# Wider vector instructions and more Strassen tiles in a fused attention and ELU feed-forward kernel

## The chip, the cores and the metric

One core of a Trainium2 chip runs the whole program. The metric is the device time of one execution in microseconds (us); the kernel before takes 332.08 us (median of 3 runs, 331.69 to 332.18).

The engines have short names in the profile: PE is TensorE's matmuls, PEld its weight loads, DVE VectorE, ACT ScalarE, POOL GpSimd, SP SyncE. PSUM is the memory that matmuls write to, SBUF the on-chip memory that all engines read.

## What is computed

Attention over 8 batches with 8 heads of 576 tokens, 64 wide. 16 beacon keys and values per head stand ahead of the 576 keys; every query sees the beacons, and the rest causally. The heads' outputs are then 4608 rows of 512, which go through a feed-forward block with an ELU between two matrix products.

```python
k_all = np.concatenate([beacon_k, k], axis=2)      # 16 + 576 keys
scores = scale * np.matmul(q, k_all.transpose(0, 1, 3, 2))
scores = np.where(causal, -1000000000.0, scores)
a = np.exp(scores - scores.max(-1, keepdims=True))
a /= a.sum(-1, keepdims=True) + 1e-09
x = np.matmul(a, v_all)                            # -> (4608, 512)
h = x @ w_in                                       # 512 x 2048, "FFN1"
g = np.where(h > 0.0, h, np.exp(np.minimum(h, 0.0)) - 1.0)
out = g @ w_out                                    # 2048 x 512, "FFN2"
```

## The kernel before, in words

**Steps and their order.** The kernel is a set of small functions ("steps") and one long list of words written out by hand at the end: `F.4.10` calls step F with the arguments 4 and 10. Each step issues a few instructions, and every engine executes its own in the order of the list. Nothing reorders them. A wait on another engine stops what stands behind it on the same engine.

**Attention.** Batch b's keys are cut in 5 chunks of 128 (the last has 80 rows). Step S (L317) computes transposed scores for a piece of columns of one batch, x (L332) takes their exp on ScalarE into the fp16 tile `et`, m (L337) multiplies the diagonal blocks by a triangle on VectorE. `et` holds two heads of one pair p, and two pairs share one buffer. For most groups D (L390) adds the chunks of `et` into one sum per head, so that L (L374, L416) needs one matmul with a vector of ones per head for the softmax denominators. n takes 1/sum on ScalarE by Ln and Exp, W (L374) multiplies with the values, M (L468) scales and writes the transposed activations `xT`. Scores of batches 0 to 2 come by transposes on TensorE (T, L263, copied out by cq and ck, L276), those of later batches by DMA transposes (lt) of a copy in DRAM (lk). Copies and loads that convert (q, k, v, w_in, w_out) are issued on POOL, where step lp also writes a memset (L773) and a copy. The four loads of w_out are the steps wo.0 to wo.3 (L163).

**Feed-forward tiles.** Tokens go in tiles: tile 0 is tokens 0 to 255, tile 1 is 256 to 511, tiles 2 to 9 have 512 tokens each. FFN1 for a block of 128 hidden features (two blocks in tiles 0 and 1) is step F (L508): four matmuls of 512 columns, or eight of 256. ELU is three steps: e (exp, ScalarE, L518), u (relu, on ScalarE at L524, or with `.v` on VectorE at L526), k (VectorE, L536), which writes `min(exp - 1, relu)` into `gt`. r and g are another form of it on VectorE (L543, L548).

**FFN2.** For tiles 2 to 9 it is a Strassen product: 7 products in place of 8 block products, at the cost of block sums. wt forms differences of w_out once, Z (line 578 through the helper `sub`) forms four block sums of `gt` per tile, Q (L624) issues some of the tile's 112 matmuls of 256 columns, J (L633, L638, L640) adds partial results and starts the output's DMA on SP. For tiles 0 and 1, FFN2 is direct: G (L557) with 512-column matmuls, 64 in all, o (L564) copies, s (L570) writes out. The last copies of tile 9 are step Jh (L744): one half by ScalarE, the other by VectorE.

**FFN1 of tiles 8 and 9** is Strassen as well, for 12 of 16 feature blocks: H forms sums of w_in (through `sub`), X sums of `xT`, P (L694) issues one product of a group of four blocks (4 matmuls), K (L704, L707) moves partial results, E, U and V (L716, L723, L733) are the ELU. The four remaining blocks of each tile go by F.

**Buffers.** PSUM has two slots for each of the names S (scores, value products, denominators), hps (FFN1) and ops (FFN2). `gt` has four half-tile buffers.

Of the kernel before, what the change touches and what calls it, by code (L numbers as in the profile page):

```python
# [8 lines left out]
FP32 = mybir.dt.float32  # L9
FP16 = mybir.dt.float16  # L10
# [7 lines left out]
def kernel(  # L18
# [66 lines left out]
    gpool = ctx.enter_context(tc.tile_pool(name="gpool", bufs=4))  # L85
# [93 lines left out]
    qks = [konst.tile([P, 2, P * NKC], BF16, name=f"qk{i}") for i in range(2)]  # L179
# [163 lines left out]
    def m(b, p, g):  # L343

        t = et(b, p)
        if b > 0:
            m_ = lambda c: triu[:, c:c + 2, :].unsqueeze(1).broadcast_to([P, 2, 2, P])
            if g == 0:
                mask(t[:, :, 0:2 * C1].rearrange("p h (j c) -> p h j c", j=2)[:, :, :, 0:P], m_(0))
            else:  # L350
                n_ = C3 - C2
                mask(t[:, :, C2 - n_ + P:C3 + P].rearrange("p h (j c) -> p h j c", j=2)[:, :, :, n_ - P:n_], m_(1))
                mask(t[0:kc[4], :, C4:ECOLS], triu[0:kc[4], 1:3, 0:ECOLS - C4])
            return
        c0, c1 = GW * g, GW * (g + 1)
# [25 lines left out]

    @step
    def D_(b, p, n, eng="v"):

        r_ = presum[b, p] = qks[p % 2].bitcast(FP16)[:, :, 0:S]
        t = et(b, p)
# [3 lines left out]
        (nc.vector if eng == "v" else nc.gpsimd).tensor_tensor(  # L390
# [7 lines left out]
    def L(b, g):  # L398
# [12 lines left out]
        else:  # L411
            t = hd[b, g] = psum.tile([P, 1024], FP32, tag="S", name="lt")
            r_ = lt[b, g] = t[:, 512 - QA:512 - QA + S]
            if (b, 2 * g) in presum:
                for i in range(4):
                    nc.tensor.matmul(  # L416
                        out=r_[32 * i:32 * (i + 1), QA:S], lhsT=ones,
                        rhs=presum[b, 2 * g + i // 2][:, i % 2, QA:S], start=True, stop=True, skip_group_check=True)
# [76 lines left out]
    hp, eb, rb, gh, ob = {}, {}, {}, {}, {}  # L495
# [54 lines left out]
    @step  # L550
    def G(t, tb_, qd):

        if qd == 0:
            ob[t, tb_] = psum.tile([P, DM], FP32, tag="ops", name="ops")
        gt = gh[t, 0].rearrange("p u (n w) -> p (u n) w", n=2)
        for fc in range(4 * qd, 4 * qd + 4):
            nc.tensor.matmul(  # L557
                out=ob[t, tb_], lhsT=gt[:, fc, P * tb_:P * (tb_ + 1)], rhs=w_out16[:, fc, :],
                start=(fc == 0), stop=(fc == NFC - 1))

    @step
    def o(t, tb_):
        osb = melt.tile([P, DM], FP32, tag="osb", name="osb")
        nc.vector.tensor_copy(out=osb, in_=ob[t, tb_])  # L564
        ob[t, tb_] = osb

    @step
    def s(t, tb_):
        row = tiles[t][0] + tb_ * P
# [369 lines left out]
```

## Time and profile before

| | |
|---|---|
| median of the runs | 332.08 us |
| the profiled execution | 331.68 us, its span 330.0 us |
| TensorE busy | 321.8 us |
| VectorE busy | 291.2 us |
| ScalarE busy | 275.0 us |
| GpSimd busy | 85.0 us |

The span runs from the first instruction of the profiled execution to the last; the 1.7 us beyond it lie around it. A row that groups instructions gives the line of the code, engine and operation, the tile written and the tiles read, the shape, the count, then busy time in us and mean ns of one, then the idle time of the engine ahead of them and what ended it. Matmuls are pipelined: the ns of one is its latency, and their pace is read from how many start in a stretch.

### The profile page before, as it was taken

How to read it: one execution, taken by the hardware profiler on the slowest of the kernel's cores; microseconds unless marked ns; L12 is line 12 of the kernel's file. 1: busy time of each engine (PE TensorE's matmuls, PEld its weight loads, DVE VectorE, ACT ScalarE, POOL GpSimd, SP SyncE). 2: the span in 40 equal slices, each digit the busy share in tenths (PEclk: the TensorE clock that was granted, in tenths of full speed). 3: DMA queues.
4: the chain of work that ended last, by engine and by line, in shares of the span. 5: the costliest groups of instructions: out<-in, count | busy, mean ns of one | idle time of the engine just before them, and what ended most of it. 6: DMA issues, size and time to landing. Idle time of an engine off the chain costs nothing.

```text
span 330.0 us, 8747 instructions
## 1 busy us (share of the span) xinstructions
PE 321.8 (98%) x3576; PEld 209.5 (63%) x3576; DVE 291.2 (88%) x614; ACT 275.0 (83%) x446; POOL 85.0 (26%) x109
## 2 busy tenths in 40 slices
PE   8989999999999999999999999999999999999995
PEld 4657766444555656556566665556656888788884
DVE  3866897899899999999989999999998899999962
ACT  1999988999889988998999999878778787888730
POOL 8861659638317009103500230000000000000000
PEclk9999999999999999999999999999999999999999
DMA  9999799999999989998995591010200011010122
GB/s 118 170 178 204 105 191 171 166 154 175 144 147 176 173 98 116 151 135 118 124 149 108 101 105 65 2 34 18 79 3 33 33 66 34 32 66 32 35 97 96
DMA packets 130009, 34.65 MB, mean 105 GB/s; under 512 B 112816, under 2 KB 129456, under 8 KB 129968
## 3 DMA queue, kind: packets, MB, share of 16 engines
q0 software_dynamic: 95840, 18.49, 68.4%
q1 hardware_dynamic: 33408, 15.34, 24.0%
q8 instruction: 28, 0.46, 0.6%
q10 hardware_dynamic: 720, 0.26, 0.3%
q14 instruction: 13, 0.11, 0.1%
HBM read 37.22 MB, written 15.34 MB: 159 GB/s over the span
## 4 chain that ended last, share of the span: by engine, by line
PE 82%; ACT 11%; DVE 3%; issue 1%; DMA 1%; ACTq 0%; DVEq 0%
PE hps L508 28%; PE ops L624 25%; ACT et L332 7%; PE sc L317 6%; PE hps L694 6%; PE ut L374 6%; PE ops L557 4%; PE sx L624 2%; ACT e L518 2%; PE lt L374 2%; DMA lo<-in_beacon_k_dram 1%; ACT r L524 1%; DVE qk L390 1%; PE lt L416 1%; PE tp L263 1%
## 5 line engine op out<-in xcount | busy, mean ns | idle before, releaser
L508 PE MATMUL hps<-xT,w_in 128*128 128x512 f16 (+1 forms) x544 | 118.7, 355 | 0.5 <-DVE r L526 0.2
L332 ACT ACTIVATE et<-sc 128x1024 f16<-128x1024 f32 (+2 forms) x114 | 105.4, 988 | 11.4 <-PE sc L317 10.9
L624 PEld LDWEIGHTS <-gt 128*128 128x128 f16 x768 | 73.7, 98 | 19.2 <-issue 2.5
L518 ACT ACTIVATE e<-hps 128x512 f32<-128x512 f32 x120 | 72.6, 621 | 10.5 <-PE hps L508 7.1
L536 DVE SCALAR_TENSOR_TENSOR gt<-e,r 128x512 f16<-128x512 f32 x112 | 75.5, 684 | 4.2 <-ACT r L524 2.5
L508 PEld LDWEIGHTS <-w_in 128*128 128x128 f16 x544 | 50.1, 98 | 41.8 <-issue 5.1
L524 ACT ACTIVATE r<-hps 128x512 f16<-128x512 f32 x88 | 54.2, 623 | 6.6 <-PE hps L508 6.1
L624 PE MATMUL ops<-w_out,gt 128*128 128x256 f16 x368 | 47.9, 273 | 0.0
L624 PE MATMUL ops<-wt,gt 128*128 128x256 f16 x352 | 47.2, 273 | 0.0
L149 POOL DMA_DIRECT2D v<-in_v_dram x40 | 36.7, 1056 | 5.5 <-issue 4.4
L337 DVE TENSOR_TENSOR et<-et,triu 128x512 f16<-128x512 f16 (+4 forms) x108 | 31.7, 332 | 3.5 <-ACT et L332 3.5
L578 DVE TENSOR_TENSOR gt<-gt 128x1024 f16<-128x1024 f16 x48 | 32.0, 684 | 0.5
L390 DVE TENSOR_TENSOR qk<-qk,et 128x416 f16<-128x416 f16 (+2 forms) x66 | 23.7, 367 | 0.7
L374 PEld LDWEIGHTS <-v 128*32 128x32 f16 (+1 forms) x800 | 17.6, 96 | 10.2 <-issue 2.8
L144 POOL DMA_DIRECT2D v<-in_beacon_v_dram x8 | 6.8, 856 | 63.9 <-PE ops L624 25.5
L374 PE MATMUL ut<-et,v 128*32 128x464 f16 (+3 forms) x560 | 21.1, 296 | 0.0
L468 DVE TENSOR_TENSOR xT<-ut,rl 128x672 f16<-128x672 f32 (+12 forms) x26 | 16.5, 671 | 4.5 <-ACT rl L434 3.4
L526 DVE TENSOR_SCALAR r<-hps 128x512 f16<-128x512 f32 x24 | 16.4, 686 | 3.4 <-ACT e L518 3.3
L733 DVE SCALAR_TENSOR_TENSOR gt<-e,r 128x512 f16<-128x512 f32 x24 | 16.1, 685 | 0.6 <-ACT e L716 0.3
L640 DVE TENSOR_TENSOR osb<-ops,sm 128x512 f32<-128x512 f32 x23 | 15.7, 683 | 1.0 <-PE ops L624 1.0
L557 PE MATMUL ops<-w_out,gt 128*128 128x512 f16 x64 | 16.2, 380 | 0.0
L624 PE MATMUL ops<-w_out,s 128*128 128x256 f16 x112 | 15.0, 273 | 0.0
(113 smaller groups left out, 413.2 us busy)
## 6 DMA issues: line engine op xcount, KB each, us to landing
out_dram<-osb SPq DMA_DIRECT2D x35, 256.0 KB, 2.3
v<-in_v_dram POOLq DMA_DIRECT2D x24, 128.0 KB, 8.0
scr<-in_q_dram POOLq DMA_DIRECT2D x5, 576.0 KB, 14.6
scr<-in_k_dram POOLq DMA_DIRECT2D x5, 576.0 KB, 14.0
w_in<-in_moe_w_in_dram POOLq DMA_DIRECT2D x8, 256.0 KB, 9.0
w_out<-in_moe_w_out_dram POOLq DMA_DIRECT2D x4, 512.0 KB, 9.8
qst<-in_q_dram POOLq DMA_DIRECT2D x4, 288.0 KB, 5.9
kst<-in_k_dram POOLq DMA_DIRECT2D x4, 288.0 KB, 7.0
```

The lines of the kernel that those rows point to most:

```text
L149: nc.gpsimd.dma_start(out=vt[b][r0:r0 + n, j, :, :], in_=v[b, :, ilo[j]:ilo[j] + n, :].rearrange("h s d -> s h d"),)
L332: nc.scalar.activation(out=ets[b, d][:, :, a - EC2 * d:e - EC2 * d], in_=sc[b, g][:, :, a - c0:e - c0], func=AFT.Exp, bias=0.0, scale=SCALE)
L337: nc.vector.tensor_tensor(out=o, in0=o, in1=i, op=ALU.mult)
L374: nc.tensor.matmul(out=t[32 * i:32 * (i + 1), a - qa:e - qa], lhsT=ones[0:kc[j], :] if half is None else v16[0:kc[j], j, h, half:D:2], rhs ...
L390: (nc.vector if eng == "v" else nc.gpsimd).tensor_tensor(out=o, in0=t[0:rows, :, a:e] if n == 0 else o, in1=t[0:rows, :, col:col + e - a], ...
L508: nc.tensor.matmul(out=h[:, n_, :], lhsT=w_in16[:, cc, P * fc:P * (fc + 1)], rhs=xt[k][:, cc, a - TT * k:e - TT * k], start=(cc == 0), sto ...
L518: nc.scalar.activation(out=eb[t, i], in_=flat(hp[t, i]), func=AFT.Exp, bias=0.0, scale=1.0)
L524: nc.scalar.activation(out=rb[t, i], in_=flat(hp[t, i]), func=AFT.Relu, bias=0.0, scale=1.0)
L536: nc.vector.scalar_tensor_tensor(out=half(t, i), in0=eb[t, i], scalar=1.0, in1=rb[t, i], op0=ALU.subtract, op1=ALU.min)
L557: nc.tensor.matmul(out=ob[t, tb_], lhsT=gt[:, fc, P * tb_:P * (tb_ + 1)], rhs=w_out16[:, fc, :], start=(fc == 0), stop=(fc == NFC - 1))
L578: (nc.vector if eng == "v" else nc.gpsimd).tensor_tensor(out=o_, in0=a_, in1=b_, op=op_)
L624: nc.tensor.matmul(out=xy[t, n_][:, qd, :], lhsT=lw[:, P * qd:P * (qd + 1)], rhs=wt_[:, c, :], start=(first and c == 0 and (qd == 0 or (t, ...
```

## The change

1. **Masks** (m, for batches from 1) and **chunk sums** (D) work on four heads at once: both pairs of a buffer are seen as one tile with four heads, and the sum goes to one tile `qkp` of four rows in place of two tiles. Half as many instructions, each twice as wide.
2. **Block sums** (Z) take a whole tile with the argument `B` (16 blocks, 2048 elements a partition) in place of two halves. Tile 9 keeps halves. `gt` gets two whole-tile buffers in place of four half-tile ones.
3. **FFN2 of tiles 0 and 1** becomes one Strassen tile: their `gt` are the two halves of one buffer, and steps Z.1, Q.1 and J.1 treat it as tile 1. Steps G, o and s are gone.
4. **FFN1 of tiles 8 and 9** is Strassen for all 16 blocks (a fourth group, g = 3). Its sums of w_in lie in a buffer of `last`, which is free after batch 7's scores. The F steps of these two tiles are gone.
5. Tile 9's first output block lies in **two PSUM tiles**, one per half, in place of one tile of two banks. J.9 works on the halves, Jh reads one tile each.
6. The whole **order** is written anew. More relus stand on VectorE (29 in place of 24 in FFN1), all four w_out loads stand together behind lp.3.1 and batch 1's values, and Q.1 starts after batch 1's attention, where G.0.0.0 stood within batch 1's scores.

```diff
-    gpool = ctx.enter_context(tc.tile_pool(name="gpool", bufs=4))
+    gpool = ctx.enter_context(tc.tile_pool(name="gpool", bufs=2))
...
-    qks = [konst.tile([P, 2, P * NKC], BF16, name=f"qk{i}") for i in range(2)]
+    qkp = konst.tile([P, 4, P * NKC], BF16, name="qkp")
+    qks = [qkp[:, 2 * i:2 * i + 2, :] for i in range(2)]
...
-            m_ = lambda c: triu[:, c:c + 2, :].unsqueeze(1).broadcast_to([P, 2, 2, P])
+            t = et4(b, p)
+            m_ = lambda c: triu[:, c:c + 2, :].unsqueeze(1).broadcast_to([P, 4, 2, P])
...
+    def et4(b, d):
+        et(b, 2 * d)
+        return ets[b, d].rearrange("p h (a c) -> p (h a) c", a=2)
...
-    def D_(b, p, n, eng="v"):
+    def D_(b, d, n):
-        r_ = presum[b, p] = qks[p % 2].bitcast(FP16)[:, :, 0:S]
-        t = et(b, p)
+        r_ = presum[b, d] = qkp.bitcast(FP16)[:, :, 0:S]
+        t = et4(b, d)
...
     def half(t, i):
-        k = t, i // UN
-        if k not in gh:
-            gh[k] = gpool.tile([P, UN, 512], FP16, tag="g", name="gt")
-        return gh[k][:, i % UN, :]
+        k = t // 2 if t < 2 else t
+        if k not in gw:
+            gw[k] = gpool.tile([P, 2 * UN, 512], FP16, tag="g", name="gt")
+            for h_ in range(2):
+                gh[(h_, 0) if t < 2 else (t, h_)] = gw[k][:, UN * h_:UN * (h_ + 1), :]
+        return gh[t, i // UN][:, i % UN, :]
...
-    def G(t, tb_, qd):
...
     def A(t, h_, j, i):
-        v_ = gh[t, h_].rearrange("p (c j) (i w) -> p c j i w", j=2, i=2)
+        if t == 1:
+            c = slice(0, NPR) if h_ == "B" else slice(HP * h_, HP * (h_ + 1))
+            return gw[0].rearrange("p (i c) (j w) -> p c j i w", i=2, j=2)[:, c, j, i, :]
+        v_ = (gw[t] if h_ == "B" else gh[t, h_]).rearrange("p (c j) (i w) -> p c j i w", j=2, i=2)
...
     def Z(t, n, h_, eng="v"):
-        c = slice(HP * h_, HP * (h_ + 1))
+        c = slice(0, NPR) if h_ == "B" else slice(HP * h_, HP * (h_ + 1))
...
     def Q(t, k0, k1):
                 if (t, n_) == (len(tiles) - 1, 0):
-                    xy[t, n_] = psum.tile([P, 2, 512], FP32, tag="S", name="sx")[:, :, 0:HM]
+                    xy[t, n_] = [psum.tile([P, 2, 512], FP32, tag="S", name="sx")[:, 0, 0:HM] for _ in range(2)]
...
+    last = stq[1][0].bitcast(FP16)
...
     def Jh(t, q_):
-        (nc.vector.tensor_copy if q_ else nc.scalar.copy)(out=osb, in_=xy[t, 0][:, q_, :])
+        (nc.vector.tensor_copy if q_ else nc.scalar.copy)(out=osb, in_=xy[t, 0][q_])
...
-    x.9.1 ...
```

Two pieces of the order, before (-) and after (+), first around w_out's loads and the first FFN2 work, then at the join of tiles 8 and 9:

```diff
-    T.1.2.0 u.0.5.v k.0.5 x.1.2 wi.3 wo.0 F.1.1 T.1.3.0 cb.2.0 ck.1.2.0 e.1.1 cq.1.3.0 u.1.1
...
-    k.0.4 G.0.0.0 lp.3.0 F.1.5 m.1.0.1 x.1.8 S.1.12 cb.2.2 e.1.6 S.1.10 G.0.1.0 m.1.2.1 u.1.6.v
...
+    m.1.1.1 T.2.2.0 ck.2.0.0 u.1.5.v ck.2.2.0 m.1.1.0 wo.1 e.1.5 m.1.0.1 F.1.6 wo.3 k.0.7 L.1.1
+    L.1.0 wo.0 F.1.2 e.1.6 wo.2 k.1.5 lk.3.0 u.1.6.v lk.3.1 F.1.4 cb.2.1 cb.2.2 n.1.1 M.1.1.0
...
+    e.2.13 x.2.8 F.2.9 u.2.12 cq.2.3.0 S.2.3 e.2.12 k.2.13 S.2.1 e.2.9 wt.1.0 k.1.2 x.2.3 F.2.2
+    e.2.2 lv.2.0.1 Z.1.3.B Q.1.0.7 x.2.1 Q.1.7.14 u.2.9.v S.2.2 S.2.0 u.2.2 k.2.12 F.2.6 k.2.9
...
-    U.9.2.6 V.9.2.6 u.9.15 Q.8.91.98 F.9.13 e.9.15 U.9.2.4 k.9.15 Q.8.98.105 J.8.5 u.9.13
-    E.9.2.4 Q.9.0.7 Q.8.105.112 V.9.2.4 Z.9.3.1 e.9.13 J.8.6 k.9.13 Z.9.1.1 Q.9.7.14 Q.9.14.21
...
+    K.9.3.5 U.9.3.4 E.9.3.4 V.9.3.1 P.9.3.6 Q.8.91.98 V.9.3.4 E.9.3.5 U.9.3.5 U.9.3.6 Z.9.1.0
+    Q.8.98.105 Q.8.105.112 J.8.6 Q.9.0.7 E.9.3.6 V.9.3.5 Z.9.3.1 V.9.3.6 Z.9.1.1 Q.9.7.14
```

More of the change, by code (lines that the diff above doesn't have):

```diff
@@ L352, in m @@
                 mask(t[:, :, C2 - n_ + P:C3 + P].rearrange("p h (j c) -> p h j c", j=2)[:, :, :, n_ - P:n_], m_(1))
-                mask(t[0:kc[4], :, C4:ECOLS], triu[0:kc[4], 1:3, 0:ECOLS - C4])
+                mask(t[0:kc[4], :, C4:ECOLS], triu[0:kc[4], 1:2, 0:ECOLS - C4].broadcast_to([kc[4], 4, ECOLS - C4]))
             return
+        t = et(b, p)
         c0, c1 = GW * g, GW * (g + 1)
@@ L548, in g @@
         nc.vector.tensor_tensor(out=half(t, i), in0=flat(hp[t, i]), in1=rb[t, i], op=ALU.max)
-    @step
-    def G(t, tb_, qd):
[L553 to L569, printed above, removed]
-        nc.sync.dma_start(out=out[row:row + P, :], in_=ob[t, tb_])
     def A(t, h_, j, i):
-        v_ = gh[t, h_].rearrange("p (c j) (i w) -> p c j i w", j=2, i=2)
+        if t == 1:
+            c = slice(0, NPR) if h_ == "B" else slice(HP * h_, HP * (h_ + 1))
+            return gw[0].rearrange("p (i c) (j w) -> p c j i w", i=2, j=2)[:, c, j, i, :]
+        v_ = (gw[t] if h_ == "B" else gh[t, h_]).rearrange("p (c j) (i w) -> p c j i w", j=2, i=2)
         return v_[:, :, j, i, :]
@@ L609, with half_of, both @@
           (0, None, B12, False), (1, (1, 0), B22, False), (0, (1, 1), T4, False)]
+    def half_of(y, q_):
+        return y[q_] if isinstance(y, list) else y[:, q_, :]
+    def both(y):
+        return [(q_, y[q_]) for q_ in range(2)] if isinstance(y, list) else [(slice(0, 2), y)]
     @step
```

283 lines of the change are left out of this document (143 added, 140 removed).

## The prediction

> **What bounds the kernel now.** I read the page first: busy times, the slices, the chain that ended last. Columns are busy time, share of the span, instructions; a digit is the tenth of a slice in which the engine was busy.
>
> ```profile
> span 330.0 us, 8747 instructions
> PE 321.8 (98%) x3576; PEld 209.5 (63%) x3576; DVE 291.2 (88%) x614; ACT 275.0 (83%) x446; POOL 85.0 (26%) x109
> PE   8989999999999999999999999999999999999995
> DVE  3866897899899999999989999999998899999962
> ACT  1999988999889988998999999878778787888730
> PE 82%; ACT 11%; DVE 3%; issue 1%; DMA 1%; ACTq 0%; DVEq 0%
> ```
>
> TensorE is busy everywhere and carries 82% of the chain. But VectorE shows nines almost throughout too, so a stage can change hands. The busy time by stretches (length, then PE, PEld, DVE, ACT, POOL with their counts, granted clock, DMA share, GB/s) says where:
>
> ```profile
> 0.00:45.00 45.00, 41.44 (x711) 28.20 (x712) 31.46 (x86) 36.52 (x51) 29.16 (x49) 1.00 1.22 158
> 100.00:220.00 120.00, 119.48 (x1280) 72.30 (x1279) 116.20 (x254) 111.22 (x178) 27.37 (x32) 1.00 1.07 113
> 263.00:297.00 34.00, 34.00 (x323) 28.18 (x321) 33.42 (x59) 27.67 (x53) 0.00 (x0) 1.00 0.14 48
> 257.30:316.90 59.60, 59.60 (x540) 49.34 (x539) 56.29 (x98) 47.07 (x89) 0.00 (x0) 1.00 0.15 50
> ```
>
> The clock is 1.00 in all of them. In the first 45 us no engine is full; the chain in time (start, length, what) shows who leads there:
>
> ```profile
> 8.99 10.11 ACT et L332 x13
> 42.64 1.84 ACT et L332 x2
> 44.53 0.70 PE tp L263 x24
> ```
>
> ScalarE's score exponentials lead from 8.99 us until batch 1's last one frees the PSUM for batch 2's transposes at 44.5 us. From there the chain is TensorE's with few breaks. In 263 to 297 VectorE has 0.58 us of idle time in 34: there two engines are full at once. This is the place to watch.
>
> **TensorE's term.** Five pieces of the chain in time give the pace of back-to-back matmuls:
>
> ```profile
> 79.93 1.73 PE ops L557 x8
> 241.40 1.73 PE hps L508 x8
> 238.25 1.53 PE ops L624 x14
> 161.77 1.63 PE ops L624 x14
> 259.42 0.87 PE hps L694 x8
> L557 PE MATMUL ops<-w_out,gt 128*128 128x512 f16 x64 | 16.2, 380 | 0.0
> L624 PEld LDWEIGHTS <-gt 128*128 128x128 f16 x768 | 73.7, 98 | 19.2 <-issue 2.5
> ```
>
> A 512-column matmul costs 1.73 / 8 = 216 ns (the 380 ns of its group is latency), a 256-column one 1.53 / 14 or 0.87 / 8 = 109 ns, 116 where a block of them follows other work. FFN2 of the first 512 tokens loses the 64 matmuls of L557, 64 x 216 = 13.8 us, and gains one Strassen tile of 112, 12.2 us. FFN1 in the last two tiles loses eight steps of L508 with four matmuls each, 32 x 216 = 6.9 us, and gains two Strassen groups of 28, 56 x 109 = 6.1 us. Net: 13.8 - 12.2 + 6.9 - 6.1 = **2.4 us less**. At 116 ns for the first tile it would be 1.6; I take 2.4, since the 14 pieces of 256 columns on the chain are at 1.53 oftener than at 1.63, and keep 1.6 for the range. Scores, exponentials, value products and warm-up matmuls are the same in number and shape. No stall is taken away by the edit itself: the gain exists only while TensorE stays full.
>
> Each of these matmuls has its own weight load of 98 ns, and 109 ns leaves no room for it in series, so it is hidden. The Trainium skill speaks against this (TensorE: Matmul & The Clock Gate, "Part 3: Packing small matmuls", what overlaps and what doesn't): weight loads overlap running matmuls only when the row group differs, and these all use the full array. By it the smaller matmuls would carry their loads openly; what that gives is a rival below. The rows above disagree with it.
>
> **VectorE's term.** Fixed cost and slope come from wide and narrow rows of the same operation, the spacing from three in a row:
>
> ```profile
> L578 DVE TENSOR_TENSOR gt<-gt 128x1024 f16<-128x1024 f16 x48 | 32.0, 684 | 0.5
> L337 DVE TENSOR_TENSOR et<-et,triu 128x512 f16<-128x512 f16 x56 | 23.2, 417 | 1.4 <-ACT et L332 1.4
> 315.53 1.90 DVE L578 TENSOR_TENSOR gt<-gt 128x1024 f16<-128x1024 f16 x3
> L707 DVE TENSOR_TENSOR kst<-hps,kst 128x512 f32<-128x512 f32 x9 | 6.2, 687 | 1.3 <-ACT kst L704 1.0 <-ACT e L716 0.3
> L564 DVE COPY osb<-ops 128x512 f32<-128x512 f32 x4 | 2.7, 686 | 0.1
> L578 DVE TENSOR_TENSOR w_in<-w_in 128x256 f16<-128x256 f16 x6 | 1.5, 283 | 0.0
> ```
>
> Slope: (684 - 417) / 512 = 0.52 ns an element; fixed part 684 - 534 = 150 ns. But three follow each other in 1.90 us, so each starts 608 ns after the last and 76 ns of the fixed part are hidden under the neighbour. Two instructions joined into one save only 150 - 76, about 70 ns. Joined pairs: 28 wide masks, 14 narrow ones, 44 chunk sums, 28 block sums in tiles 2 to 8; 114 x 70 = **8.0 us less**. The wider rows themselves are not in the trace; below they are bounded by nothing saved, above by the whole 150 ns (17 us). I take 70, the spacing row.
>
> The Trainium skill has a rule on this too (VectorE: DVE Perf Modes, "Terms", DRAIN): the next operation can't issue until the pipeline is empty. By it a joined pair would save the full 150 ns, 17 us in all, and rival A below would fall away. The 1.90 us row disagrees.
>
> Added on VectorE: four block sums of 2048 elements for the first tile (68 + 1067 = 1.14 us each, 4.5); six additions like L707 (3.6 at 0.6 us spacing); eight pair sums of w_in at 0.2 (1.6); 7 more instructions in the outputs of FFN2, less the four copies of L564 (4.2 - 2.4 = 1.8); by the new order five more relus on VectorE (3.0). Sum 14.5 added, 8.0 saved: **VectorE has about 6.5 us more work in all**. Most of the saving falls between 60 and 230 us, most of the additions before 100 and after 240. Between 100 and 220 it has 3.8 us of idle time now and gets lighter there, so I charge nothing; if that cover went, it would cost what VectorE had over TensorE.
>
> After 257 us it is otherwise. From the first Strassen matmul of tile 8 to the third product of tile 9's FFN2:
>
> ```profile
> 257.29 0.60 PE L694 MATMUL hps<-xT,w_in 128*128 128x256 f16 x4
> 316.89 2.08 PE L624 MATMUL sx<-wt,gt 128*128 128x256 f16 x16
> ```
>
> Before, these 59.6 us hold 56.29 of VectorE. Between the same two points the new order has six more additions and eight more Strassen ELU steps (14 x 0.6 = 8.4) and eight more w_in sums (1.6), and eight fewer plain ELU steps and two fewer others (-6.0): 4.0 us more, 60.3. TensorE's own share there grows by 14 Strassen products of 0.44 us, less eight F steps of 0.86, plus two pieces of FFN2 of 0.77: 59.6 + 0.7 = 60.3. So the two are level, and VectorE has its idle time on top. The nearest row is the full stretch, 0.58 in 34, 1.0 us in 60: the stage takes 61.3, and **TensorE waits 1.0 us**. The ends: 0 if TensorE covers it, 3.3 if VectorE idles as much as before (59.6 - 56.29).
>
> **ScalarE** gets six more copies, five fewer relus and one output copy; the sum is within 1 us in 275, and it is not full after 220. At the start it leads: the new order puts 1.1 us less of its work ahead of the last exponential of batch 1 (two relus fewer) and leaves TensorE 1.0 us less from batch 2's transposes on, together 2.1 less where TensorE alone would have 2.4. **Start: +0.3 us**; the ends are -1.5 and +1.5, since filling matmuls are reordered (Strassen starts later than L557 did).
>
> **The tail.**
>
> ```profile
> 324.05 1.91 PE L624 MATMUL sx<-wt,gt 128*128 128x256 f16 x16
> 326.00 0.37 ACT L744 COPY osb<-sx 128x256 f32<-128x256 f32 x1 [4.66 <-PE sx L624]
> 326.40 0.42 DVE L744 COPY os<-sx 128x256 f32<-128x256 f32 x1 [1.46 <-ACT osb L744]
> ```
>
> VectorE's copy of the second half waits for ScalarE's of the first, as both read one tile. With two tiles ScalarE's copy starts after the first eight of the 16 matmuls, VectorE's at the end of the last: **0.4 us less**. Splitting costs two short instructions earlier, off the path.
>
> **New waits and moved DMAs.** A block sum over 16 blocks waits for all ELU steps of its tile; behind it on VectorE stand later ELU steps, for which TensorE's next PSUM bank waits. In the new order each stands behind the last ELU step of its tile, so nothing is charged. The first ELU step of tile 3 waits for the last matmul of the first Strassen tile, since they share a buffer; it stands behind it in the order. Four output DMAs take the place of four of the same size on SP. On POOL all four loads of w_out now stand together behind batch 1's values and a memset that waits for a transpose:
>
> ```profile
> 36.15 0.18 POOL L773 MEMSET qst<- 128x96 bf16 x1 [9.55 <-PE tp L263]
> DMA to landing us min/median/max: 6.2/9.8/13.1
> ```
>
> That memset ran at 36.15 us. From it six loads of v and four of w_out, at about 0.8 us of issue each, put the last issue near 44 and its landing at 54 to 57; the first difference of w_out on VectorE comes near 60 by the sums of work ahead of it. Charged nothing, with 3 us to spare.
>
> **Sum:** -2.4 (matmuls) + 0.3 (start) + 1.0 (VectorE at the end) - 0.4 (tail) = -1.5. Against the profiled execution, 331.68 us for its span of 330.0: 330.2. The median of the runs is 0.4 higher, 332.08, so **330.6 us**.
>
> **The rivals.** A: *VectorE sets the pace of the last two tiles* with its idle time of now, 3.3 us, instead of 1.0: 332.9, and slower than before as soon as the stage takes over 63.5 us. For it: both engines full in 263 to 297. Against it: ELU steps of two groups can fill each other's gaps. B: *w_out lands late*: VectorE stops at the first w_out difference, and all behind it. With the longest landing, 13.1 us after 44, it decides as soon as the memset comes 3 us later than now; at 6 us the loss is 3: 333.6. For it: the memset already waited 9.55 us; against it: less work stands ahead of its transpose. C: *weight loads of 98 ns in the open*: 112 x 207 - 64 x 314 and 56 x 207 - 32 x 314 ns add 3.1 + 1.5 in place of -2.4: 337.6. Against it: 109 ns in the rows above. It is what the Trainium skill's rule on weight loads, named above, would make of the change. D: *the joined instructions don't do what they should*, running at 1.04 ns an element as the f32 rows do (687 for 512): the 28 masks alone add 28 x 1024 x 0.52 = 15 us, over 10 beyond the idle time there: above 340. Against it: the mask row runs at 0.52 with the same kind of broadcast. E: *the new order fills the start better* and TensorE covers the end: -2.4 - 1.5 - 0.4, 327.8.
>
> **How the numbers follow.** Forecast 54% (329.2 to 331.4); A 20%, half of it within 0.2% of now; E 17%; B 5%; D 3%; C 1%. A measurement can tell about 0.2%, 0.7 us, from no change. Faster: nearly all of the forecast and E, 68%; within: 13%; slower: 19%. The range, 327.9 to 333.2, takes in E's end and A, and leaves B, C, D.
>
> **What would show it.** The first Strassen matmuls of tile 8 should come near 254.5 us (257.3 less the earlier matmuls); from there to the third product of tile 9 near 61 us with VectorE over 97% busy; block sums of 2048 at 1.2 us, four-head masks at 0.68; FFN2 blocks of 14 still at 1.53 to 1.63; the last VectorE copy within 0.1 us of the last matmul. A PE idle of more than 2 us after 255 us, or VectorE waiting on a w_out load, would prove the forecast wrong.

## The result, and the profile after

The changed kernel takes 329.94 us (median of 4 runs, 329.65 to 330.35) where the kernel before takes 331.88 us beside it (331.68 to 332.18): a ratio of 0.9942, 95% interval 0.9924 to 0.9959. The forecast was 330.6 us. Measured once more, on another chip, it is 330.86 against 332.25 us, 0.9955 (0.9934 to 0.9975). The ratios leave out runs that count as slow, over 1.5% above the fastest of the same kernel; only one kernel of this document has such runs (v early, three of twelve), and its median counts them.

The page of the changed kernel answers to the lines shown of before:

```profile
span 328.2 us, 8827 instructions
PE 318.5 (97%) x3648; PEld 215.7 (66%) x3648; DVE 296.9 (90%) x527; ACT 276.4 (84%) x449; POOL 85.2 (26%) x109
PE 72%; DMA 12%; ACT 7%; POOL 4%; DVE 3%; issue 2%; DVEq 0%; POOLq 0%
```

VectorE has 87 instructions fewer and 5.7 us more to do (291.2 before). The chain has a part it hardly had: 12% of DMA for 1%, and by the page's list of lines 10% of the span are loads of v. The stretches, with the same columns as before:

```profile
0.00:45.00 45.00, 40.13 (x712) 27.67 (x712) 31.44 (x77) 36.64 (x50) 33.17 (x53) 1.00 1.39 167
100.00:220.00 120.00, 119.22 (x1276) 71.64 (x1274) 114.41 (x196) 109.21 (x173) 28.01 (x33) 1.00 1.01 108
263.00:297.00 34.00, 34.00 (x339) 29.79 (x337) 33.32 (x55) 29.89 (x58) 0.00 (x0) 1.00 0.16 53
255.26:315.60 60.34, 60.34 (x578) 53.19 (x576) 59.12 (x101) 50.31 (x97) 0.00 (x0) 1.00 0.13 45
```

The last row is the stage of tiles 8 and 9 between the two points that the prediction named; VectorE is busy 59.12 of its 60.34 us (98%), and TensorE without a break. Two of the wider instructions, from the groups, and a piece of the chain of work that shows the pace of the 256-column matmuls:

```profile
L566 DVE TENSOR_TENSOR gt<-gt 128x2048 f16<-128x2048 f16 x24 | 29.2, 1217 | 0.1
L338 DVE TENSOR_TENSOR et<-et,triu 128x1024 f16<-128x1024 f16 x28 | 18.9, 682 | 0.6 <-ACT et L333 0.5
```

```profile
242.29 1.53 PE ops L618 x14
```

A block sum of 2048 takes 1.22 us, a four-head mask 0.68, and 14 matmuls 1.53 us, 109 ns each, as before. The points themselves, in the timeline of TensorE, and the tail in that of all engines:

```profile
255.26 0.60 PE L706 MATMUL hps<-xT,w_in 128*128 128x256 f16 x4
315.60 1.99 PE L618 MATMUL sx<-wt,gt 128*128 128x256 f16 x16
322.66 1.91 PE L618 MATMUL sx<-wt,gt 128*128 128x256 f16 x16
323.74 0.37 ACT L756 COPY osb<-sx 128x256 f32<-128x256 f32 x1 [3.78 <-PE sx L618]
324.61 0.43 DVE L756 COPY os<-sx 128x256 f32<-128x256 f32 x1 [1.05 <-PE sx L618]
```

VectorE's last copy now waits for TensorE, not for ScalarE, and starts 0.04 us after the last matmul ends at 322.66 + 1.91 = 324.57. So the 1.8 us by which the span became shorter are made up as follows:

| stretch | before | changed | difference | forecast |
|---|---|---|---|---|
| to the first Strassen matmul of tile 8 | 257.29 | 255.26 | -2.0 | -2.8 |
| from there to the third product of tile 9 | 59.60 | 60.34 | +0.7 | +1.7 |
| from there to the end of the span | 13.1 | 12.6 | -0.5 | -0.4 |

The sum is right within 0.3 us, but the first two rows are off by 0.8 and 1.0 us in opposite directions. That is what the experiments are about.

### The profile page after: what moved, and what is told of

It reads as the page before. It is cut to its first block, busy times and chain, and to the rows that moved or that the text cites. A ratio compares the mean times of both kernels' runs of the same rounds, so it can differ in the third digit from the quotient of the medians.

```text
span 328.2 us, 8827 instructions
## 1 busy us (share of the span) xinstructions
PE 318.5 (97%) x3648; PEld 215.7 (66%) x3648; DVE 296.9 (90%) x527; ACT 276.4 (84%) x449; POOL 85.2 (26%) x109
## 4 chain that ended last, share of the span: by engine, by line
PE 72%; DMA 12%; ACT 7%; POOL 4%; DVE 3%; issue 2%; DVEq 0%; POOLq 0%
PE ops L618 27%; PE hps L514 22%; DMA v<-in_v_dram 10%; PE hps L706 8%; PE sc L318 5%; ACT et L333 5%; PE ut L376 5%; PE sx L618 2%; POOL scr L769 1%; POOL v L149 1%; DMA kst<-in_k_dram 1%; ACT e L524 1%; POOL w_out L163 1%; DVE qkp L396 1%; PE lt L422 1%
## 5 line engine op out<-in xcount | busy, mean ns | idle before, releaser
L514 PE MATMUL hps<-xT,w_in 128*128 128x512 f16 (+1 forms) x512 | 110.7, 353 | 0.3 <-DVE gt L556 0.3
L618 PEld LDWEIGHTS <-gt 128*128 128x128 f16 x864 | 83.0, 98 | 21.1 <-issue 2.9
L618 PE MATMUL ops<-w_out,gt 128*128 128x256 f16 x416 | 54.7, 273 | 0.0
L618 PE MATMUL ops<-wt,gt 128*128 128x256 f16 x400 | 53.6, 273 | 0.0
L530 ACT ACTIVATE r<-hps 128x512 f16<-128x512 f32 x74 | 45.0, 616 | 4.5 <-PE hps L514 4.3
L566 DVE TENSOR_TENSOR gt<-gt 128x2048 f16<-128x2048 f16 (+1 forms) x30 | 33.1, 1110 | 0.1
L338 DVE TENSOR_TENSOR et<-et,triu 128x1024 f16<-128x1024 f16 (+4 forms) x66 | 26.6, 447 | 1.8 <-ACT et L333 1.7
L396 DVE TENSOR_TENSOR qkp<-qkp,et 128x1344 f16<-128x1344 f16 (+2 forms) x33 | 19.2, 583 | 0.4
L716 ACT COPY kst<-hps 128x512 f32<-128x512 f32 x24 | 13.9, 589 | 4.8 <-PE hps L706 4.6
L618 PEld LDWEIGHTS <-s 128*128 128x128 f16 x144 | 13.9, 98 | 2.5
```

What stands on the lines that cost most here:

```text
L338: nc.vector.tensor_tensor(out=o, in0=o, in1=i, op=ALU.mult)
L396: nc.vector.tensor_tensor(out=o, in0=t[0:rows, :, a:e] if n == 0 else o, in1=t[0:rows, :, col:col + e - a], op=ALU.add)
L514: nc.tensor.matmul(out=h[:, n_, :], lhsT=w_in16[:, cc, P * fc:P * (fc + 1)], rhs=xt[k][:, cc, a - TT * k:e - TT * k], start=(cc == 0), sto ...
L530: nc.scalar.activation(out=rb[t, i], in_=flat(hp[t, i]), func=AFT.Relu, bias=0.0, scale=1.0)
L566: (nc.vector if eng == "v" else nc.gpsimd).tensor_tensor(out=o_, in0=a_, in1=b_, op=op_)
L618: nc.tensor.matmul(out=half_of(xy[t, n_], qd), lhsT=lw[:, P * qd:P * (qd + 1)], rhs=wt_[:, c, :], start=(first and c == 0 and (qd == 0 or ...
```

## The experiments

The theory: TensorE's fewer columns (-2.4) and the tail (-0.4) are the gain, VectorE stays hidden, and something ahead of tile 8 takes 0.8 us. Rivals: the gain came from the wider vector instructions; VectorE sets the pace of the last two tiles; the changed start and order made it.

The runs of one kernel scatter by 2 us and more on the chips of these groups, so effects below 1 us are read from the traces by four points: the first value product of batch 2 (a), the first Strassen matmul of tile 8 (b), the third product of tile 9 (c) and the end of the span (d). The clock is TensorE's granted clock from 24 to 28 us, from the stretches.

| kernel | a | a to b | b to c | c to d | clock | median, us | ratio to before |
|---|---|---|---|---|---|---|---|
| before | 84.78 | 172.51 | 59.59 | 13.1 | 1.00 | 331.88 | |
| before, again | 85.30 | 172.52 | 59.57 | 13.1 | 1.00 | 331.91 | 1.0006 (0.9986 to 1.0025) |
| changed | 82.36 | 172.90 | 60.34 | 12.6 | 1.00 | 329.94 | 0.9942 (0.9924 to 0.9959) |
| changed, again | 84.60 | 172.87 | 60.35 | 12.6 | 0.61 | 330.86 | 0.9955 (0.9934 to 0.9975) |
| one tail tile | 82.50 | 172.59 | 60.35 | 13.0 | 1.00 | 331.05 | 0.9971 (0.9942 to 1.0001) |
| FFN2 direct first | 84.41 | 173.33 | 60.34 | 12.6 | 1.00 | 332.40 | 1.0022 (1.0000 to 1.0044) |
| last group direct | 82.72 | 172.85 | 60.96 | 12.5 | 1.00 | 330.71 | 0.9964 (0.9943 to 0.9985) |
| vector more | 82.49 | 173.19 | 61.78 | 12.6 | 1.00 | 332.51 | 1.0024 (1.0007 to 1.0042) |
| pairs apart | 84.91 | 174.89 | 60.35 | 12.5 | 0.57 | 331.77 | 0.9982 (0.9957 to 1.0007) |
| v early | 82.89 | 177.10 | 60.35 | 12.5 | 1.00 | 334.40 | 1.0050 (1.0021 to 1.0079) |
| no r | 83.97 | 172.35 | 60.35 | 12.6 | 0.69 | 330.80 | 0.9943 (0.9918 to 0.9967) |
| v early, no r | 83.67 | 172.12 | 60.35 | 12.6 | 0.65 | 330.40 | 0.9930 (0.9903 to 0.9957) |
| v early, relu on ScalarE | 83.98 | 172.75 | 60.60 | 12.6 | 0.64 | 330.73 | 0.9963 (0.9930 to 0.9997) |
| v early, no r, warm | 83.69 | 172.11 | 60.34 | 12.6 | 1.00 | 330.61 | 0.9957 (0.9939 to 0.9975) |

The stage from b to c repeats within 0.02 us in all but one of the kernels that leave it alone (60.60 with the relus on ScalarE); point a does not. Each ratio is to the runs of before beside it. After the first measurement there were four groups, each on one chip: one tail tile, direct first, last group and v early; changed again, no r, v early with no r and pairs apart; before again, vector more and the version with relus on ScalarE; the warm one alone.

**The tail.** Undone alone:

```diff
-xy[t, n_] = [psum.tile([P, 2, 512], FP32, tag="S", name="sx")[:, 0, 0:HM] for _ in range(2)]
+xy[t, n_] = psum.tile([P, 2, 512], FP32, tag="S", name="sx")[:, :, 0:HM]
```

> The changed kernel with tile 9's first output block in one tile of two PSUM banks again, so that VectorE's last copy waits for ScalarE's. Theory: the end comes 0.37 us later, as long as ScalarE's copy: 330.3 us against 329.94. Rival: the end is set by the DMA of the other half, which ScalarE starts: no difference, 329.9 us.

Its timeline of the end:

```profile
322.49 1.91 PE L618 MATMUL sx<-wt,gt 128*128 128x256 f16 x16
324.44 0.37 ACT L756 COPY osb<-sx 128x256 f32<-128x256 f32 x1 [4.65 <-PE sx L618]
324.85 0.42 DVE L756 COPY os<-sx 128x256 f32<-128x256 f32 x1 [1.46 <-ACT osb L756]
```

VectorE's copy starts 0.45 us after the last matmul (324.40) in place of 0.04, and the stretch to the end is 13.0 in place of 12.6 us. The 0.4 us are the tail's. By the median alone, 331.05 with an interval up to 1.0001, it could not be told.

**FFN2 of the first 512 tokens direct again:**

```diff
-    Z.1.3.B Q.1.0.7 x.2.1 Q.1.7.14 u.2.9.v
+    G.0.0.0 x.2.1 G.0.0.1 u.2.9.v
...
-    Q.1.105.112 k.2.0
+    G.1.1.3 k.2.0 o.1.1 s.1.1 wt.3.0 wt.3.1
```

> The changed kernel with FFN2 of the first 512 tokens direct again: 16 pieces of four 512-column matmuls (G) stand where the 16 pieces of seven Strassen matmuls (Q.1) stood, its block sums and additions are gone, and the third difference of w_out is formed after the last of them. Theory (the gain is TensorE's fewer columns): 64 x 216 - 112 x 109 = 1.6 us are lost: 331.5 us against the changed kernel's 329.94. Rival (the gain came from the wider vector instructions and the new order, the Strassen tile itself is neutral): VectorE loses some 4.5 us of work before 100 us and the time is 329.9 us or less.

It takes 332.40 us, 1.4 us more than the kernel beside it that has only the old tail, whose own loss is 0.4: about 1.8 us, where the columns give 1.6. The intervals are wide for such a sum, but the gain as a whole is gone: the ratio is 1.0022 (1.0000 to 1.0044). In the traces it reaches tile 8 2.5 us later than the changed kernel (257.74 for 255.26). The rival falls: VectorE lost work and the kernel became slower.

**The last feature group of tiles 8 and 9 by F again**, without its eight sums of w_in:

```diff
-    P.9.3.0 U.9.2.4 E.9.2.6 Q.8.49.56 U.9.2.5.v V.9.2.4 K.9.3.0 J.8.3 P.9.3.1 P.9.3.2
+    U.9.2.4 E.9.2.6 Q.8.49.56 F.9.12 U.9.2.5.v V.9.2.4 J.8.3 F.9.13 e.9.12 u.9.12
```

> The changed kernel with the fourth feature group of tiles 8 and 9 done by F steps again, its sums of w_in and its additions gone. Theory (TensorE covers VectorE in the last two tiles, its columns set the pace): 32 x 216 - 56 x 109 = 0.8 us are lost: 330.7 us against 329.94. Rival (VectorE sets the pace there, being busy 59.1 of the 60.3 us): it loses 6 additions, 8 pair sums and some ELU work, over 3 us in all, and the time falls below 329.5 us.

```profile
255.56:316.53 60.97, 60.97 (x555) 50.86 (x552) 54.87 (x87) 47.09 (x91) 0.00 (x0) 1.00 0.13 44
```

The stretch from b to c shows VectorE (third after the length) with 54.87 us, 4.2 less than in the changed kernel, and the stage is 0.6 us longer, not shorter. TensorE's 0.8 us of columns are lost, and 0.2 come back, from where isn't broken down. VectorE doesn't set the pace there.

**How near VectorE is**, by four relus of tile 9 moved to it from ScalarE:

```diff
-    V.9.0.1 U.9.0.6 Z.8.3.B
+    V.9.0.1 U.9.0.6.v Z.8.3.B
...
-    J.7.6 U.9.0.4 P.9.1.1
+    J.7.6 U.9.0.4.v P.9.1.1
...
-    K.9.1.5 U.9.1.4 E.9.1.4
+    K.9.1.5 U.9.1.4.v E.9.1.4
...
-    P.9.2.2 U.9.1.5 Q.8.56.63
+    P.9.2.2 U.9.1.5.v Q.8.56.63
```

> The changed kernel with four relus of tile 9 (U.9.0.4, U.9.0.6, U.9.1.4, U.9.1.5) moved from ScalarE to VectorE: 4 x 0.6 = 2.4 us more for VectorE in the stretch from the first Strassen matmul of tile 8 to tile 9's third product, which has 59.1 of its 60.3 us busy on VectorE. Theory (TensorE stands just above VectorE there): VectorE's 1.2 us of idle time are used up and 1 to 2.4 us come on top of the stage, 61.3 to 62.7 us, the kernel about 331 to 332. Rival (VectorE's wait is nowhere near, its idle time can be filled): the stage stays at 60.3 and the time as the changed kernel's.

```profile
255.67:317.46 61.79, 60.89 (x579) 53.21 (x577) 60.64 (x105) 48.90 (x93) 0.00 (x0) 1.00 0.13 44
```

The stage is 61.78 us, 1.4 longer, about what VectorE's busy time grew by (1.5; three of the four read SBUF and take 0.42 us). It has 60.64 of 61.79 us now, its idle time is what it was (1.2 us), and TensorE has 0.9 us of breaks. So VectorE's 1.2 us were not filled, and for work added at these four places the changed kernel stands at the very point from which it is paid in full; other places were not tried.

**Masks and chunk sums on two heads at a time:**

```diff
-            t = et4(b, p)
-            m_ = lambda c: triu[:, c:c + 2, :].unsqueeze(1).broadcast_to([P, 4, 2, P])
+            m_ = lambda c: triu[:, c:c + 2, :].unsqueeze(1).broadcast_to([P, 2, 2, P])
+            for t in (et(b, 2 * p), et(b, 2 * p + 1)):
...
+        for i in range(2):
+            t = et(b, 2 * d + i)
+            o = r_[0:rows, i::2, a:e]
```

> The changed kernel with masks and chunk sums on two heads at a time again, each joined instruction as two in a row, all else as changed: 86 more VectorE instructions, at 70 ns each 6.0 us more work between 30 and 230 us. Theory (TensorE sets the pace there, VectorE has its idle time, 5.6 us of it between 100 and 220): 0 to 1 us later than the changed kernel, most of it before 130 us. Rival (the joined instructions are what the change lives on): the whole gain of 1.9 us or more is lost, 331.9 us or above.

A group row of the changed kernel (that of its masks stands above), then those of this one:

```profile
L396 DVE TENSOR_TENSOR qkp<-qkp,et 128x1344 f16<-128x1344 f16 x11 | 9.3, 848 | 0.1
```

```profile
L338 DVE TENSOR_TENSOR et<-et,triu 128x512 f16<-128x512 f16 x56 | 21.9, 414 | 0.1
L398 DVE TENSOR_TENSOR qkp<-qkp,et 128x672 f16<-128x672 f16 x22 | 10.1, 496 | 0.0
```

A joined mask replaces two of 414 ns by one of 682. Where the next instruction follows at once, it starts 335 ns after one of a pair and 602 ns after a joined one (medians of all such places in the two traces): 2 x 335 - 602 = 68 ns saved, and 68 for the chunk sums of 1344 (2 x 418.5 - 769). The forecast's 70 ns holds. In time the kernel is 0.9 us slower than the changed one beside it (331.77 for 330.86), inside what the theory allowed. Its trace has 2.0 us more from a to b, but it is that of the slowest of its twelve runs, 334.40 us. Up to one us of that is not the pairs' own work, but a single instruction of VectorE's, of a kind that usually takes 0.43 us and that the next experiments explain:

```profile
126.25 1.43 DVE L553 TENSOR_SCALAR r<-e 128x512 f16<-128x512 f32 x1
```

The wider instructions take no work off TensorE, but without them the ratio to before is 0.9982 (0.9957 to 1.0007) in place of 0.9955: by the medians most of the gain is lost, and the rival that all of it is lost is not excluded. The matmuls' gain is there only as long as VectorE stays out of their way.

**The loads of v.** The wait that the trace of the changed kernel shows ahead of tile 8 is that of batch 2's value product, in TensorE's timeline:

```profile
82.36 0.38 PE L376 MATMUL ut<-et,v 128*32 128x464 f16 x4
83.00 1.31 PE L376 MATMUL ut<-et,v 128*32 128x464 f16 x36 [0.26 <-DMA v<-in_v_dram]
```

After its first four matmuls it stands until a load of v lands. In the new order that load is issued behind a copy of batch 4 and loads of batch 3. Moved ahead of these:

```diff
-    lv.2.2.3.4 u.1.4 M.1.0.1 lk.4.0 e.1.2 lv.3.2.3.4 ... e.2.2 lv.2.0.1 Z.1.3.B
+    lv.2.2.3.4 lv.2.0.1 u.1.4 M.1.0.1 lk.4.0 e.1.2 lv.3.2.3.4 ... e.2.2 Z.1.3.B
```

> The changed kernel with one word of the order moved: the last two value loads of batch 2 (step lv.2.0.1) are issued right behind lv.2.2.3.4, ahead of lk.4.0 and lv.3.2.3.4, not behind them. Its median is to be set against the changed kernel's 329.94 us. Theory: the value product of batch 2 waited for these loads (TensorE stood 0.29 and 0.57 us near 82 us, where the chain of work holds 15.7 us of this load), and nothing else was late there, so TensorE gets the 0.8 us back that it lost between 60 and 100 us: 329.1 us. Rival: the loads only hide another wait (VectorE or ScalarE late at the same place, or another load that is now pushed back), so the time stays at 329.9 us.

Here my theory fell: 334.40 us, *above* the changed kernel (a ratio to before of 1.0050 for 0.9942, about 3.6 us) and slower than before. The wait for v is gone, and in its place TensorE waits 3.0 us for VectorE, by the waits from 80 to 90 us. After it the granted clock (third column from the right) falls:

```profile
PE ops L618 <- DVE wt L566: 3.0, 1, 3.0
```

```profile
84.00:88.00 4.00, 1.04 (x21) 0.66 (x14) 4.00 (x5) 1.45 (x3) 3.73 (x4) 1.00 2.41 154
88.00:92.00 4.00, 3.99 (x24) 1.84 (x24) 4.00 (x10) 3.12 (x5) 3.03 (x5) 0.67 2.32 172
92.00:96.00 4.00, 4.00 (x81) 2.21 (x79) 2.40 (x5) 2.75 (x4) 0.00 (x0) 0.90 2.27 173
```

The clock costs 0.33 x 4 + 0.10 x 4 = 1.7 us more. Wait and clock together, less the wait for v that is gone, are about the 4.2 us by which a to b has grown (177.10 for 172.90). The runs spread from 330.47 to 336.93 us, so the stall need not be the same in each. VectorE's timeline and GpSimd's of the same kernel say why TensorE waited:

```profile
81.55 0.68 DVE L544 SCALAR_TENSOR_TENSOR gt<-e,r 128x512 f16<-128x512 f32 x1
82.15 4.02 DVE L551 TENSOR_SCALAR r<-e 128x512 f16<-128x512 f32 x1
86.09 0.67 DVE L544 SCALAR_TENSOR_TENSOR gt<-e,r 128x512 f16<-128x512 f32 x1
```

```profile
81.50 2.20 POOL L769 DMA_DIRECT2D scr<-in_k_dram  x1 [9.24 <-issue]
83.19 2.72 POOL L769 DMA_DIRECT2D scr<-in_q_dram  x1
84.86 2.74 POOL L149 DMA_DIRECT2D v<-in_v_dram  x2
```

One r step, an instruction of 427 ns by its median, took 4.02 us, while GpSimd issued one DMA after the other. r is the only kind that reads f32 from SBUF and writes SBUF with one tensor input in this part of the program; the additions, masks and ELU steps beside it keep their durations. The steps of this kind, by count and min/median/max, first in before and then in the changed kernel:

```profile
L543 DVE TENSOR_SCALAR r<-e x8: 414/420/428, 207.8 to 243.6; 128x512 f16<-128x512 f32 x8
```

```profile
L551 DVE TENSOR_SCALAR r<-e x9: 412/427/1020, 30.1 to 168.2; 128x512 f16<-128x512 f32 x9
```

Before, all eight stand behind 207 us, when GpSimd has no DMA left to issue. The new order puts nine between 30 and 168 us, and one of them, at 105.6 us, is 0.6 us longer than its kind, while GpSimd issues five loads of v from 104.68 to 109.52. The rows of the changed kernel, VectorE's and GpSimd's:

```profile
105.60 1.02 DVE L551 TENSOR_SCALAR r<-e 128x512 f16<-128x512 f32 x1 [1.20 <-ACT e L524]
```

```profile
104.68 4.84 POOL L149 DMA_DIRECT2D v<-in_v_dram  x5
```

The Trainium skill has the rule (SBUF — State Buffer, "Who interferes with whom"): a tensor_scalar can run in a mode that uses both of VectorE's SBUF ports, one pair of which it shares with GpSimd, and whoever comes first blocks the other entirely. The traces agree, with 1.02 and 4.02 in place of 0.43 us; the page warns of VectorE holding up GpSimd's DMA issue, here it is the other way round. But not every r step beside an issue is held up, and a long one need not last until the issues end (that of 1.02 us ended at 106.62, that of 4.02 us at 86.17 with loads issued until 87.60). In the trace of vector more one stands within the issue of a copy and takes its usual time, VectorE's row and GpSimd's:

```profile
113.48 0.41 DVE L551 TENSOR_SCALAR r<-e 128x512 f16<-128x512 f32 x1
```

```profile
113.27 2.39 POOL L769 DMA_DIRECT2D scr<-in_k_dram  x1 [1.16 <-DMA scr<-in_k_dram]
```

What part of an issue holds it stays open.

**Without r steps in tiles 2 and 3**, first in the changed kernel, then in the one with v ahead:

```diff
-    Q.1.84.91 r.2.3 k.2.11
+    Q.1.84.91 u.2.3.v k.2.11
...
-    L.2.1 g.2.3 J.1.5
+    L.2.1 k.2.3 J.1.5
...
-    r.3.12 g.3.12 F.3.15
+    u.3.12.v k.3.12 F.3.15
...
```

> The changed kernel with the five r/g pairs of tiles 2 and 3 (r.2.3, r.3.2, r.3.12, r.3.15, r.3.0) made the other form of the same ELU, u on VectorE and k. Each pair costs VectorE 0.27 us more (685 for 414 ns). Theory (an r step stands still while GpSimd issues a DMA): the 0.6 us of the r step at 105.6 us, which lies on the chain, goes, and the runs in which another meets a DMA near 82 us: 0.4 to 0.8 us below the changed kernel beside it, and less scatter. Rival (VectorE's work between 60 and 130 us is what counts, and the long r step only filled a wait): 5 x 0.27 us more VectorE work, same time or up to 1 us later.

> The kernel with the two value loads of batch 2 moved ahead, which took 334.4 us, with the same five r/g pairs made u on VectorE and k. Theory: in that kernel the r step at 82.15 us took 4.02 us, as long as GpSimd issued two copies of batch 5 and its loads; without it 3.6 us come back, and the time is 330 us or a little less. Rival (the moved loads push other transfers, and the long r step only waited for the same thing as everybody): 333 us or more.

The second shows the r step to be the cause: 330.40 in place of 334.40 us (0.9930 for 1.0050), and 172.12 in place of 177.10 from a to b, though VectorE has more to do and GpSimd issues the same DMAs at the same place:

```profile
81.12 2.20 POOL L769 DMA_DIRECT2D scr<-in_k_dram  x1 [8.69 <-issue]
82.82 2.72 POOL L769 DMA_DIRECT2D scr<-in_q_dram  x1
84.49 2.75 POOL L149 DMA_DIRECT2D v<-in_v_dram  x2
```

The first takes 330.80 us beside 330.86, a miss by the medians (the runs are set side by side by their clock below); in the trace a to b is 0.5 us shorter than in either trace of the changed kernel. With v ahead as well, 0.2 more.

> The changed kernel with batch 2's value loads ahead and the five r/g pairs of tiles 2 and 3 made u on ScalarE and k on VectorE. Against the version with u on VectorE, VectorE has 5 x 0.69 = 3.4 us less and ScalarE 5 x 0.5 = 2.5 us more between 80 and 130 us. Theory (no r step meets a DMA issue, and VectorE, not ScalarE, is short there): 0.9 us or more below the changed kernel, 329.0 us on a chip like the first. Rival (ScalarE's exponentials of batches 3 and 4 are as short of time): as the changed kernel or slower.

With the five relus on ScalarE the time is 330.73 us, and a to b 0.6 us longer than with them on VectorE. The stretch from 100 to 220 us of the two, first with them on VectorE:

```profile
100.00:220.00 120.00, 119.67 (x1285) 71.66 (x1282) 115.20 (x194) 109.16 (x172) 27.38 (x33) 1.00 1.00 107
```

```profile
100.00:220.00 120.00, 119.46 (x1283) 71.50 (x1282) 112.00 (x189) 110.27 (x175) 27.36 (x33) 1.00 0.99 107
```

VectorE gave up 3.2 us and ScalarE has 1.1 more, and TensorE is a little less busy: nothing came of it. The theory's number missed; the rival's fits, though ScalarE's 110 of 120 us don't show it full.

**The start.** Again the two kernels as they are:

> The kernel before as it is, for its trace on the same chip as the others of this group. Expected: 331.9 us. The first two traces had TensorE busy 41.44 us (before) and 40.13 us (changed) of the first 45, and the prediction priced the start at 0.3 us. If that price is a matter of the order, the changed kernels of this group stand 0.9 to 1.3 us behind this one in TensorE's busy time of the first 45 us; if it is the scatter of the first loads, the sign changes from chip to chip.

> The changed kernel as it is, once more, to see how far its time scatters on one chip and to stand beside the three others of this group. Expected: 329.9 us by the first measurement. Where the runs scatter by more than 1 us, as those of the first group did, the theory of the shared stall (VectorE's r step, L551, which is 427 ns by its median and 1020 ns at 105.6 us, while GpSimd issues loads) expects the slow ones to have a longer r step near 82 us.

The kernel before is as expected. The changed one is not in all: point a comes at 84.60 us where it was 82.36, and no r step is long near 82 us; the only one that stands out much is that near 106 us again (1.02 us at 107.83; 0.60 to 1.02 us in every trace of this order that has an r step there). What differs is the granted clock (third column from the right), here in this trace and then in the first one of before:

```profile
20.00:24.00 4.00, 2.31 (x81) 1.67 (x74) 2.41 (x4) 2.25 (x3) 2.11 (x5) 0.97 1.58 192
24.00:28.00 4.00, 4.00 (x30) 2.28 (x34) 2.77 (x12) 3.02 (x4) 2.32 (x5) 0.61 1.29 204
```

```profile
20.00:24.00 4.00, 2.95 (x76) 1.96 (x69) 2.56 (x9) 3.35 (x5) 1.65 (x3) 1.00 1.53 187
24.00:28.00 4.00, 3.78 (x74) 2.82 (x75) 1.88 (x8) 4.00 (x8) 1.88 (x3) 1.00 1.37 198
```

In the new order TensorE has 1.9 to 2.8 us of work from 20 to 24 us, and in five of eleven traces without the extra warm-up its clock falls afterwards, in all four of one chip among them; point a then comes 1 to 2.5 us later (83.7 to 84.9, against 82.4 to 82.9 in the others but for the direct version). A clock of 0.61 for 4 us is 1.6 us of TensorE's time. The mean granted clock of each run, from its record, says the same where there is no trace: of changed again, the seven runs with 0.998 or more took 330.05 to 330.93 us, the five with 0.995 or less 331.56 to 332.40. But on that chip 8 of the 31 runs of the kernel before have 0.995 or less too (333.37 to 335.03 us, the others 331.14 to 333.02), and of pairs apart, which has the changed kernel's order, only 1 of 12. So the clock goes with much of the scatter, and that the new order is what lowers it is not shown.

On the chip where the kernel before was traced again, vector more kept its clock and had 40.51 us of TensorE's work in the first 45, before 41.33: 0.8 us less, where 0.9 to 1.3 were expected of an effect of the order. Twenty-two warm-up matmuls more:

```diff
-    W.0.A.0 S.0.1.1
+    W.0.A.0 wx.10 S.0.1.1
...
         for i, src in enumerate(st[b]):
+            if (b, p, i) == (1, 1, 1):
+                wx(12)
```

> The version with batch 2's value loads ahead and no r step in tiles 2 and 3, and 22 more warm-up matmuls of 128 columns, whose results nobody reads: 10 ahead of S.0.1.1 and 12 in the middle of T.1.1.0, where TensorE stood idle for 1.5 of the 4 us from 20 to 24. In five traces of the new order the granted clock fell to 0.57 to 0.69 from 24 to 28 us, after TensorE had been busy 2.0 to 2.5 of these 4 us; in the trace of before, with 2.95, and in six others of the new order it stayed at 1.00. Theory (the idle time there lowers the clock in some runs, and that is most of the scatter of the changed kernel): clock 1.00 from 20 to 28 us, TensorE over 40.1 us busy in the first 45, the median 1 us below the version without the warm-up (330.4 us), and the slowest run nearer to it. Rival (the scatter comes from loads that land at other times): clock or not, the same median and spread, or 0.5 us later for the 22 matmuls.

```profile
20.00:24.00 4.00, 3.00 (x72) 2.33 (x62) 1.58 (x3) 1.74 (x3) 2.64 (x5) 1.00 1.47 197
24.00:28.00 4.00, 3.81 (x66) 2.57 (x70) 3.10 (x12) 3.57 (x5) 1.52 (x3) 1.00 1.29 205
```

The clock stayed at 1.00 in its trace and at 0.996 or more in all twelve runs, but the median is 330.61 us for 330.40 and the runs spread from 329.79 to 332.19. In TensorE's timeline the 12 in the middle of T.1.1.0 stand behind a stop, and so took 0.8 us of their own:

```profile
22.56 0.28 PE L277 MATMUL tp<-identb,qst 96*64 96x96 bf16 x4 [0.99 <-issue]
22.77 0.84 PE L222 MATMUL w<-lo 128*128 128x128 bf16 x12
```

A stop of 0.8 us that ends near 22.5 us, for which the profile shows no cause, is in the traces of the kernel before and of the changed one too. Point a is at 83.69 us, where it was 83.67 without the 22 matmuls and with the lower clock: what the clock gave, they may have taken. With the clock whole the runs still spread by 2.4 us, so it is not all of the scatter; what makes the rest stays open.

**The lowest ratio.** With v ahead and no r steps in tiles 2 and 3 the ratio to before is 0.9930 (0.9903 to 0.9957), the lowest of all. The intervals don't part it from the changed kernel beside it, 0.9955; its trace is 0.8 us shorter from a to d. Of the runs with a mean clock of 0.998 or more, its four took 328.68 to 329.29 us, the four without r steps alone 329.30 to 331.10, and the changed kernel's seven 330.05 to 330.93. That speaks for a gain of about 1.4 us over the changed kernel, from few runs that were sorted by their clock afterwards.

## Why the prediction was right, and where not

- **Bound and matmuls (-2.4): right.** TensorE covers, its columns count. Direct FFN2 costs about 1.8 us where 1.6 was worked out, the direct last group 0.6 where it was 0.8. Weight loads stay hidden (rival C falls): PEld is busy 53.19 of the 60.34 us, and the pace is 109 ns.
- **Start (+0.3): right in size where the clock holds, its reason not shown.** If for each matmul of the first 60 us one sums the distance to the next start less its own columns at 0.42 ns (divided by the number that run side by side), the changed kernel loses 0.3 us more than before, and vector more 0.2 more than before, again. But the term was worked out from ScalarE's lead up to batch 2's transposes at 44.5 us, and the changed kernel's chain leaves ScalarE at 32.0 us (30.99 + 1.03) and goes on over GpSimd's issues; TensorE has no idle time ahead of the transposes of batch 2 at 45.10 us, where before it stood 0.17 us for ScalarE. That the size agrees may be luck. That the clock may fall after 22 us, which costs 1 to 2 us, was in no term.
- **VectorE's term: price right, place not.** 70 ns per joined pair was measured (68), and VectorE's total rose 5.7 us for a forecast 6.5. The block sums of 2048 take 1.22 us and the four-head masks 0.68, as forecast (rival D falls).
- **VectorE's wait in the last two tiles (+1.0): the step that failed.** The sum was 60.3 us of work, "So the two are level, and VectorE has its idle time on top." VectorE has 59.1 there, 2.8 us more than before and not 4.0. Of these 1.2 us, 0.6 are the eight pairs of block sums that were joined within the stage, a saving that I had counted for the kernel but not here; 0.5 are a ninth plain ELU step and a pair sum of w_in that fell outside, less one more sum of xT inside; the rest isn't broken down. The stage took TensorE's 60.3 us without a break, so the wait was nothing where 1.0 was forecast. That VectorE is level all the same, with its 1.2 us of idle time on top of its work, the four moved relus show (+1.4 us for 1.5 us of work). So the rule was right and the sum 1.2 us too high.
- **New waits and moved DMAs (nothing): wrong by 0.8.** w_out was in time (rival B falls). The issues of its loads and the first differences in the changed kernel, with first and last start:

```profile
L163 POOL DMA_DIRECT2D w_out<-in_moe_w_out_dram x4: 790/798/808, 40.1 to 42.3; - x4
L566 DVE TENSOR_TENSOR wt<-w_out x2: 684/684/685, 58.6 to 63.0; 128x1024 f16<-128x1024 f16 x2
```

  The longest took 13.2 us to land, so the last was there by 55.5. But the same walk along GpSimd's queue, done for v, would have shown batch 2's last loads behind a copy of batch 4. And r steps were moved in time past GpSimd's DMA issues, on another engine than the one whose queue I followed. Without both, a to b is 172.1 for 172.9 us, 0.8 less, as much as the first row of the small table lacks.
- **Tail (-0.4): right**, 0.4 by undoing it.
- **Rivals.** A's mechanism shows as soon as four relus more stand on VectorE; E's end of 327.8 was reached by no median, and lies 0.1 us outside the range that is said to take it in. The two misses, +0.8 and -1.0, cancel by luck: with both right the sum would have been -1.7, against the -1.8 of the spans.

## What to carry to other kernels

When a step is moved in the order, look not only at what it waits for but at what runs beside it on GpSimd: a VectorE instruction with one f32 input from SBUF cost up to nine times its price beside GpSimd's DMA issues, and another form of the same step only 0.27 us more. An edit that only moves a load can be judged only together with such neighbours, so an experiment that goes the wrong way is worth a look at the single durations. And for two engines that are level, work out both sums in the same stage, instruction by instruction, as one us of a missed saving there is the whole difference between a wait and none.

## What the runs showed of the hardware

- One VectorE instruction (r, 128x512, f32 to f16 in SBUF) can stand still while GpSimd issues DMAs: 1.02 us beside loads of v and 4.02 us beside two copies and the loads behind them, for 0.43 alone. It doesn't always: one within the issue of a copy took 0.41. In the traces of this case no addition, mask, ELU step or relu from PSUM that recurs was more than 0.1 us above the median of its kind.
- TensorE's granted clock can fall to a mean of 0.57 to 0.69 over 4 us in the middle of a busy program after 4 us in which TensorE was 2.0 to 2.5 us busy, and did so in only some traces with such busy times (it stayed at 1.00 after 2.52 us in the changed kernel's first trace and after 1.92 in v early's). After 4 us with 1.04 us busy it fell to 0.67. The Trainium skill (TensorE: Matmul & The Clock Gate, "Part 1: The HAM clock gate") says that the gate looks at windows of time which run freely; that would make it a matter of where the break falls, and no run here separates that.
